# Direct loads by head groups in 512-byte pieces, GpSimd's loads between its constants, the last chunk stored in halves, and a new order of all steps

## The chip, the cores and the metric

The kernel runs on one core of a Trainium2 chip. The core has five engines with instruction queues of their own: TensorE (PE in the profile, with PEld for its weight loads), VectorE (DVE), ScalarE (ACT), GpSimd (POOL) and SyncE (SP). Transfers between the chip's memory and the core run on 16 DMA engines and are issued here from SP, ACT and POOL. The metric is the device time of one execution in microseconds (us).

## The reference

Causal attention over 4 batches, 8 heads, 768 positions and a head size of 64, in which three heads see all earlier positions and five see the first 4 positions and a window of 64. Its output, 3072 rows of 512, goes through a gated feed-forward layer with a gated residual:

```python
scores = scale * np.matmul(q, k.transpose(0, 1, 3, 2))
stream_keep = causal & (is_sink | in_win)
mask = np.where(retr[0, :, 0, 0, None, None], full_mask, stream_mask)
...
a = a / (np.sum(a, axis=-1, keepdims=True) + 1e-09)
x = np.matmul(a, v)            # heads put side by side: 3072 x 512
g = x @ w_gate
gelu = 0.5 * g * (1.0 + erf(g * inv_sqrt2))
ffn_out = gelu * (x @ w_val) @ w_out
res_gate = 1.0 / (1.0 + np.exp(-(x @ w_res)))
out = x + res_gate * ffn_out
```

The weights are 512 x 1536 (gate, value), 1536 x 512 (out) and 512 x 512 (res).

## The kernel before

**Stages.** The 3072 rows are worked on in six chunks of 512 (`CHUNKS`, line 25), each four tiles of 128 positions. A chunk goes through attention (scores on PE, exponentials on ACT, masks on DVE, products with the values on PE, normalization on DVE), then gate and value products (PE), GELU (ACT), their product (DVE), then the output product and the residual gate. From chunk 1 on, half of the gate and value products and all output products are Strassen-like: sums of blocks on DVE replace some matmuls. PE works in fp16 and sums in fp32. Heads are taken in pairs, `PAIRS = ((0, 2), (4, 6), (1, 3), (5, 7))`, in the order 0, 2, 1, 3 in the first chunks.

**The order is written out.** Each step is a task with an engine, the tasks that it depends on, and its buffers; the tasks are numbered as they are made. The list `PLAN` (line 51) names them by number in the order in which they enter their engines' queues, with a letter where a task may run on several engines (a: ACT, d: DVE, g: POOL), and `w34` for 34 filler matmuls on zeros (line 1468). `PLACES` gives the buffer of each. `schedule` (line 263) puts the tasks into the queues, and `assign_waits` gives each one the semaphore waits that its dependences need. Nothing is decided while the kernel runs: an engine waits where its next task is not ready.

**The front.** The numbers that matter:

- 211, 217 (SP) and 214, 220 (ACT) are the direct loads (`loads_first`, line 646): keys and queries of batch 0, positions 0 to 255, in fp32. In the kernel before, 211 and 214 bring positions 0 to 127 of all eight heads, 217 and 220 positions 128 to 255. A contiguous piece in memory is one head's row of 64 numbers, 256 bytes.
- 212, 213, 215, 216, 218, 219, 221, 222 cast them to fp16 in halves. 223, 225, 227, 229 transpose them on PE, 224, 226, 228, 230 copy the results to the tiles kT and qT.
- 417, 420, 423, 428 are the scores of pairs 0, 2, 1 and 3 of the first two tiles, and 418, 421, 424/425, 429 their exponentials (line 911).
- 231, 232 are GpSimd's loads of the keys and queries of positions 256 to 511, with their transposes and copies 245 to 252. 233 to 236 load the values, 254 a piece of the keys of batch 1.
- 2, 4 to 11 are GpSimd's nine constants: the identity (2) and two masks. Here every load from GpSimd depends on all of them (`consts` in `dma`, line 540). 12 copies a part of the window mask, 3 makes the fp32 identity. 237 to 240 copy sink values.
- 200, 202, 204 load `w_gate` in three pieces, 201, 203, 205 `w_val`, 206 `w_res`, 207 to 210 `w_out`. 507 and 490 cast attention outputs to fp16 on GpSimd. 575 is the first product that needs load 204.

In the queues before, GpSimd runs all constants, then 232, 231, 233, 234, 236, 235, 254, 200, 201, 203, the sink copies, 202, 204, 205, and so on; the casts 507 and 490 come after 206.

**The back.** Of the last chunk, `output_fast` (line 1340) runs for two pairs of tiles, `pi` 0 and 1. Each pair has two residual products with tanh (1799 to 1802 for `pi` 0), seven Strassen products, DVE's sums (`plus`; 1814, 1817, 1820), gates (`gated`, line 1409), adds of x (line 1419, DVE or GpSimd) and stores (line 1425, SP or ACT). 1821 and 1822 are the very last product; it needs sum 1817. `end` marks the pair that is gated, added and stored in halves of 256 columns: before, `pi` 1 of the last chunk alone, while the pair that finishes last in the list, `pi` 0, is added and stored in whole rows.

**xD** (line 1101) are transposing copies within the core on SP's queue, one in each of chunks 3 to 5 (1188, 1424, 1662).

Of the kernel before, what the change touches and what calls it, by code (L numbers as in the profile page):

```python
# [429 lines left out]
def build_kernel(nc, q, k, v, w_gate, w_val, w_out, w_res, out):  # L430
# [61 lines left out]
    def at16(buf):  # L492
        return at(buf).bitcast(FP16)
# [152 lines left out]
    def loads_first(b, a):  # L646
# [18 lines left out]
        for i in range(2):  # L665
            for j in (1, 0):
# [17 lines left out]
                for p in range(NPAIR):  # L684
                    (BB.ktok if j else BB.qtok)[p, a + i] = t
# [881 lines left out]
```

## Time and profile before

| what | us |
|---|---|
| median of 3 runs | 259.19 (259.07 to 259.86) |
| the profiled execution | 259.19 |
| its span, first to last instruction | 257.4 |
| PE busy | 250.4 |
| DVE busy | 203.1 |
| ACT busy | 164.7 |
| POOL busy | 105.5 |

A line of a timeline or of the page's groups gives start or count, duration, engine, the line of the kernel, the operation and its tiles, and in brackets how long the engine had been idle before and what ended that. "x16" is the number of merged instructions, and the duration is that of all of them. A window's row gives its length, then for PE, PE's weight loads, DVE, ACT and POOL the busy time and the number of instructions, then the granted clock, the share of the DMA engines and GB/s. The chain of work that ended last is followed back from the last instruction, at each step to what released it; a line of it names the engine that was waited for. Matmuls are pipelined and their ends are modelled, so that a PE that shows as busy can still be waiting a little.

### The profile page before, as it was taken

How to read it: one execution, taken by the hardware profiler on the slowest of the kernel's cores; microseconds unless marked ns; L12 is line 12 of the kernel's file. 1: busy time of each engine (PE TensorE's matmuls, PEld its weight loads, DVE VectorE, ACT ScalarE, POOL GpSimd, SP SyncE). 2: the span in 40 equal slices, each digit the busy share in tenths (PEclk: the TensorE clock that was granted, in tenths of full speed). 3: DMA queues.
4: the chain of work that ended last, by engine and by line, in shares of the span. 5: the costliest groups of instructions: out<-in, count | busy, mean ns of one | idle time of the engine just before them, and what ended most of it. 6: DMA issues, size and time to landing. Idle time of an engine off the chain costs nothing.

```text
span 257.4 us, 8048 instructions
## 1 busy us (share of the span) xinstructions
PE 250.4 (97%) x3407; PEld 176.7 (69%) x3407; DVE 203.1 (79%) x453; ACT 164.7 (64%) x298; POOL 105.5 (41%) x144
## 2 busy tenths in 40 slices
PE   8999999999999999999999999999999999999992
PEld 5657645468576668567678566689587689678881
DVE  2798344899988997577998478999687887768975
ACT  2698944986567994475977355993456997264410
POOL 8995900947862549069423086003310010210031
PEclk9999999999999999999999999999999999999999
DMA  8999999999999999999929899409997005360004
GB/s 150 170 199 206 194 198 203 162 154 106 172 154 248 179 114 125 176 247 168 147 34 162 224 138 153 29 10 83 150 154 239 3 6 84 41 84 4 3 22 144
DMA packets 104116, 33.71 MB, mean 131 GB/s; under 512 B 90768, under 2 KB 99216, under 8 KB 104080
## 3 DMA queue, kind: packets, MB, share of 16 engines
q0 software_dynamic: 72592, 18.36, 82.3%
q1 hardware_dynamic: 29120, 13.91, 28.4%
q10 hardware_dynamic: 2368, 0.92, 1.6%
q8 instruction: 27, 0.44, 0.7%
q14 instruction: 9, 0.07, 0.1%
HBM read 29.36 MB, written 10.49 MB: 155 GB/s over the span
## 4 chain that ended last, share of the span: by engine, by line
PE 93%; ACT 3%; DVE 2%; issue 1%; DVEq 0%
PE ps L477 49%; PE ps L478 32%; PE ps L895 5%; PE ps L1468 3%; PE ps L1019 2%; PE ps L1115 1%; PE ps L726 1%; PE ps L986 1%; ACT es L911 1%; ACT ea L911 1%; DVE otile L1409 1%; ACT vs L622 0%; PE ps L670 0%; DVE otile L1385 0%; DVE otile L1419 0%
## 5 line engine op out<-in xcount | busy, mean ns | idle before, releaser
L1413 POOL DMA_DIRECT2D out_dram<-otile x16 | 15.8, 1021 | 85.8 <-DVE otile L1409 55.3
L542 POOL DMA_DIRECT2D qks<-in_q_dram x35 | 33.8, 1010 | 16.6 <-issue 8.3
L542 POOL DMA_DIRECT2D qks<-in_k_dram x35 | 34.4, 1034 | 12.8 <-PE ps L726 12.8
L477 PE MATMUL ps<-xT,wg 128*128 128x512 f16 (+1 forms) x172 | 38.4, 337 | 0.0
L477 PE MATMUL ps<-xT,wv 128*128 128x512 f16 (+1 forms) x166 | 37.9, 338 | 0.0
L1183 ACT ACTIVATE gact<-ps 128x512 f16<-128x512 f32 x38 | 22.1, 595 | 23.8 <-PE ps L477 16.3
L1185 DVE SCALAR_TENSOR_TENSOR hT<-gact,ps 128x512 f16<-128x512 f16 x38 | 25.7, 684 | 11.6 <-ACT gact L1183 6.1
L1257 DVE TENSOR_TENSOR ps<-ps,otile 128x256 f32<-128x256 f32 x60 | 24.9, 431 | 9.9 <-PE ps L478 5.1
L542 POOL DMA_DIRECT2D va<-in_v_dram x24 | 24.5, 1055 | 5.1 <-PE ps L477 5.1
L477 PEld LDWEIGHTS ps<-xT,wg 128*128 128x128 f16 x172 | 16.4, 98 | 11.0 <-ACT gact L1183 0.3
L1353 ACT ACTIVATE srs<-ps 128x512 f32<-128x512 f32 x22 | 13.1, 597 | 15.3 <-PE ps L478 11.6
L477 PEld LDWEIGHTS ps<-xT,wv 128*128 128x128 f16 x166 | 15.9, 98 | 9.9 <-ACT xT L1125 0.3
L1275 ACT ACTIVATE gact<-ps 128x512 f16<-128x512 f32 x30 | 16.9, 598 | 6.7 <-PE ps L478 4.1
L911 ACT ACTIVATE ea<-ps 128x1024 f16<-128x1024 f32 (+2 forms) x24 | 21.1, 928 | 0.0
L1282 DVE SCALAR_TENSOR_TENSOR hT<-gact,ps 128x512 f16<-128x512 f16 x30 | 19.6, 680 | 1.7 <-PE ps L477 1.7
L1253 ACT ACTIVATE ps<-ps 128x256 f32<-128x256 f32 x25 | 9.2, 370 | 16.9 <-PE ps L477 12.2
L478 PE MATMUL ps<-xT,wv 128*64 128x512 f16 (+1 forms) x156 | 19.2, 341 | 0.0
L1086 DVE TENSOR_TENSOR xtok<-ps,rcp 128x512 f32<-128x512 f32 (+1 forms) x28 | 17.1, 609 | 1.0 <-ACT x L1094 0.4
L477 PE MATMUL ps<-wo,hT 128*128 128x256 f16 (+1 forms) x114 | 17.7, 296 | 0.0
L478 PE MATMUL ps<-xT,wg 128*64 128x512 f16 (+1 forms) x144 | 17.3, 344 | 0.0
L1385 DVE TENSOR_TENSOR otile<-otile,ps 128x256 f32<-128x256 f32 x33 | 13.6, 415 | 4.6 <-PE ps L478 3.6
L895 PE MATMUL ps<-qT,kT 64*128 64x64 f16 (+3 forms) x391 | 16.5, 213 | 0.7 <-ACT xT L1125 0.6
(188 smaller groups left out, 588.0 us busy)
## 6 DMA issues: line engine op xcount, KB each, us to landing
out_dram<-xtok SPq DMA_DIRECT2D x4, 1024.0 KB, 5.7
out_dram<-otile POOLq DMA_DIRECT2D x16, 256.0 KB, 4.8
va<-in_v_dram POOLq DMA_DIRECT2D x24, 128.0 KB, 6.7
qks<-in_q_dram POOLq DMA_DIRECT2D x32, 64.0 KB, 6.2
qks<-in_k_dram POOLq DMA_DIRECT2D x32, 64.0 KB, 6.4
wg<-in_moe_w_gate_dram POOLq DMA_DIRECT2D x3, 512.0 KB, 12.3
wv<-in_moe_w_val_dram POOLq DMA_DIRECT2D x3, 512.0 KB, 12.2
wo<-in_moe_w_out_dram POOLq DMA_DIRECT2D x4, 384.0 KB, 18.5
```

The source lines that it names most:

```text
L477: return e.matmul(o, lhsT=lhsT, rhs=rhs, **k)
L478: return [e.matmul(o[h:h + 64], lhsT=lhsT[:, h:h + 64], rhs=rhs, **k) for h in (0, 64)][-1]
L542: return G.add(eng, issue, lambda e: e.dma_start(out_ap(), in_ap), list(deps) + (consts if eng == "pool" else []), prio, bufs=bufs, dma=co ...
L895: return [e.matmul(at(scr)[:, oo:oo + w], lhsT=side(BB, qb, low, 1)[half, k0:k0 + 128], rhs=side(BB, qb, low, 0)[half, qq:qq + w], start=T ...
L911: return e.activation(out=o, in_=i_, func=AF.Exp, scale=SM_SCALE)
L1086: t2 = G.add("dve", c_dve(2 * n * 64), lambda e: e.tensor_tensor(out=xview(), in0=avv(0, DHEAD), in1=scale(), op=ALU.mult), [t1] + xdeps, ...
L1183: ta = G.add("act", c_act(512), (lambda gb=gb, ga=ga, gw=gw: lambda e: e.activation(out=at(ga)[:, :], in_=at(gb)[:, gw], func=AF.Gelu))(), ...
L1185: th = G.add("dve", c_dve(512), (lambda vb=vb, ga=ga, f=f, vw=vw: lambda e: e.scalar_tensor_tensor(out=hv(f), in0=at(ga)[:, :], scalar=0.5 ...
L1257: return G.add("dve", c_dve(256), lambda e: e.tensor_tensor(out=at(ps)[:, o], in0=at(ps)[:, BL], in1=at(es)[:, 0:256], op=ALU.add), deps, ...
L1275: ta = G.add("act", c_act(512), (lambda x=x, ga=ga, both=both: lambda e: e.activation(out=two(at(ga)[:, :]), in_=both(x), func=AF.Gelu))() ...
L1282: th = G.add("dve", c_dve(512), (lambda x=x, f=f, ga=ga, both=both: lambda e: e.scalar_tensor_tensor(out=two(hv(f)), in0=two(at(ga)[:, :]) ...
L1413: t = G.add("pool", 1.0, (lambda ot=ot, r0=r0: lambda e: e.dma_start(out[r0:r0 + 128, :], at(ot)[:, :], accum_op=ALU.add))(), ends + [stor ...
```

## The change

- **Direct loads.** 211 and 214 now bring heads 0 to 3 of positions 0 to 255, 217 and 220 heads 4 to 7. Two neighbouring positions of a head are one piece of 512 bytes on one partition. The transposes take every second position and the copies put them in order. On SP 211 now goes first. Scores 417 and 420 thereby depend on 211 and 214 alone, 423 and 428 on 217 and 220.
- **GpSimd.** Its loads no longer depend on the constants. The queue is 6, 7, 231, 8, 232, 2, 233, 4, 234, 9, 235, 10, 11, cast 221, 236, 5, 200, 237, 238, 201, 239, 240, 202, 203, cast 507, 264, 204, 205, ..., 254, ..., 206. Computations on GpSimd depend on the computation before them there, and its transfers on the latest xD ahead of them in the list.
- **The last chunk.** `end` holds for both pairs, so that `pi` 0 has one more gate, two more adds and two more stores (numbers from 1823 on, with 1830 to 1865 moved up by five). Two dependences of the products on tanh and on each other are gone.
- **The order.** `PLAN` and `PLACES` are new throughout. 21 fillers instead of 34 stand ahead of the first transposes, 31 instead of 47 in all. On ACT, 224, 219, 222, 12 come ahead of exponential 418, and 228, 252 and 3 are its own now; 246 has gone to DVE. At the end, 1817 is queued ahead of 1820 on DVE, and 1815, 1816 ahead of 1818, 1819 on PE.

```diff
 PLAN = (
-    "0 17 18 214 217 211 1 220 199 212a 216 6 7 15 218a 16 2 215 8 w34 225 219a 4 3 213 223 226 9 10 222 5 227 221a 228 229 "
...
+    "0 15 211 214 6 7 18 220 231 199 212a 8 232 217 17 1 213a 2 215 216a w21 223 233 225 4 16 226 224a 234 219a 9 235 222a "
...
+    "1868g 1800 1814 1823 1818 1825g 1817 1870 1819 1801 1821 1822 1820 1827 1869a 1824 1826 1802 1829 1828a 1864a 1831g "
+    "1833 1830 1832 1834a "
...
+            if e == "pool" and t.dma:
+                t.deps += [u for u in order if u.name == "xD"][-1:]
+            if e == "pool" and not t.dma:
+                t.deps += [u for u in prog[e] if not u.dma][-1:]
...
-        return G.add(eng, issue, lambda e: e.dma_start(out_ap(), in_ap), list(deps) + (consts if eng == "pool" else []), prio,
+        return G.add(eng, issue, lambda e: e.dma_start(out_ap(), in_ap), list(deps), prio,
...
-        for i in range(2):
+        for o in range(2):
             for j, src, eng in ((1, k, "sp"), (0, q, "act")):
-                ld = G.add(eng, 0.6, (lambda src=src, j=j, i=i: lambda e: e.dma_start(
-                    view(j, i, 0, 2).rearrange("p (h d) -> p h d", h=NHEAD),
-                    src[b, :, lo + 128 * i:lo + 128 * i + 128, :].rearrange("h p d -> p h d")))(),
+                ld = G.add(eng, 0.6, (lambda src=src, j=j, o=o: lambda e: e.dma_start(
+                    view(j, o, 0, 2).rearrange("p (h w) -> p h w", h=4),
+                    src[b, 4 * o:4 * o + 4, lo:lo + 256, :].rearrange("h (p i) d -> p h (i d)", i=2)))(),
...
-                    for p in range(NPAIR) for x in range(2)])(),
+                    for m, p in enumerate(ps_) for i in range(2) for x in range(2)])(),
...
-        end = c == len(CHUNKS) - 1 and pi == 1
+        end = c == len(CHUNKS) - 1
...
-        p6 = product(X, "S2", "T2", False, [k1] + (tas if end else []))
+        p6 = product(X, "S2", "T2", False, [k1])
...
-        p4 = [product(X, "A22", "T4", False, [c22] + ([p2] if end else []))]
+        p4 = [product(X, "A22", "T4", False, [c22])]
```

The copies of the sink values may now stand on GpSimd by the list instead of always, the clearing of the sink tiles and the mask products are written in the form for several engines with DVE as the only one, and the gates that read from SBUF alone have a name of their own.

More of the change, by code (lines that the diff above doesn't have):

```diff
@@ L534, in build_kernel @@
     for i, vk in enumerate(P_vk.items):
-        P_vk.last[i] = [G.add("dve", 0.5, (lambda vk=vk: lambda e: e.memset(vk[:, :, :], 0.0))(), [t_blank], -94, name="vzero")]
+        P_vk.last[i] = [G.flex({e_: (0.5, (lambda vk=vk: lambda e: e.memset(vk[:, :, :], 0.0))()) for e_ in ("dve",)}, [t_blank], -94, name="vzero")]
     for i, va in enumerate(P_v.items):
@@ L541, in dma @@
         issue = 0.85 if eng == "pool" else 1.2
-        return G.add(eng, issue, lambda e: e.dma_start(out_ap(), in_ap), list(deps) + (consts if eng == "pool" else []), prio,
+        return G.add(eng, issue, lambda e: e.dma_start(out_ap(), in_ap), list(deps), prio,
                      bufs=bufs, dma=cost, name=name, grp=grp)
     inits = [x for l in P_v.last for x in l], [x for l in P_vk.last for x in l]
-    consts = [x for x in G.tasks if x.name == "const"]
     wtok = {}
@@ L609, in values @@
                 if b == 0:
-                    t.eng, t.alts, t.prio = "pool", None, VK_AT
-                    t.dur, t.deps = 0.3, t.deps + [x for x in G.tasks if x.name == "const"]
+                    t.prio = VK_AT
+                    hs = VK[BB.vktok.index(t)]
+                    t.alts["pool"] = (0.3, vk("pool", BB.vktok.index(t), *hs))
         a_ = max(a, 1)
@@ L651, in loads_first @@
         st, half = [Buf(P_st), Buf(P_st)], [Buf(P_x16), Buf(P_x16)]
-        view = lambda j, i, o, n=1: at(st[j])[:, :].bitcast(FP32)[:, (i * 2 + o) * 256:(i * 2 + o + n) * 256]
-        h16 = lambda j, i, o, n=1: at(half[j]).rearrange("p c i k -> p (c i k)")[:, (i * 2 + o) * 256:(i * 2 + o + n) * 256]
-        for i in range(2):
+        view = lambda j, o, g, n=1: at(st[j])[:, :].bitcast(FP32)[:, (o * 2 + g) * 256:(o * 2 + g + n) * 256]
+        h16 = lambda j, o, g, n=1: at(half[j]).rearrange("p c i k -> p (c i k)")[:, (o * 2 + g) * 256:(o * 2 + g + n) * 256]
@@ L659, in loads_first @@
                     [], -60, bufs=[st[j]], dma=0.9, name="ldf")
-                for o in range(2):
-                    def cast(on, j=j, o=o, i=i):
-                        return lambda e: (e.activation(out=h16(j, i, o), in_=view(j, i, o), func=AF.Copy) if on == "act" else
-                                          e.tensor_copy(out=h16(j, i, o), in_=view(j, i, o)))
-                    tok[j, i, o] = G.flex({e: (0.4, cast(e)) for e in ("dve", "act", "pool")}, [ld], -205, bufs=[st[j], half[j]], name="c16")
@@ L665, in loads_first, with cast @@
-        for i in range(2):
+                for g in range(2):
+                    def cast(on, j=j, o=o, g=g):
+                        return lambda e: (e.activation(out=h16(j, o, g), in_=view(j, o, g), func=AF.Copy) if on == "act" else
+                                          e.tensor_copy(out=h16(j, o, g), in_=view(j, o, g)))
+                    tok[j, o, g] = G.flex({e: (0.4, cast(e)) for e in ("dve", "act", "pool")}, [ld], -205, bufs=[st[j], half[j]], name="c16")
+        for o in range(2):
+            ps_ = sorted(ORDER[2 * o:2 * o + 2])
+            assert sorted(h for p in ps_ for h in PAIRS[p]) == list(range(4 * o, 4 * o + 4))
@@ L666, in loads_first @@
             for j in (1, 0):
                 scr = Buf(P_ps, "scr0")
-                to, o0 = (BB.kt, lo + 128 * i) if j else (qb, qo + 128 * i)
-                tt = G.add("pe", 0.3, (lambda scr=scr, j=j, i=i: lambda e: [
-                    e.transpose(out=at16(scr)[64 * x:64 * x + 64, p * 128:(p + 1) * 128],
-                                in_=h16(j, i, 0, 2)[:, PAIRS[p][x] * 64:PAIRS[p][x] * 64 + 64], identity=ident[:, :])
-                    for p in range(NPAIR) for x in range(2)])(),
-                    [t_ident] + [tok[j, i, o] for o in range(2)], 80 * i - 205, bufs=[half[j], scr], name="qkT")
+                to, o0 = (BB.kt, lo) if j else (qb, qo)
@@ new lines, in loads_first @@
+                tt = G.add("pe", 0.3, (lambda scr=scr, j=j, o=o, ps_=ps_: lambda e: [
+                    e.transpose(out=at16(scr)[64 * x:64 * x + 64, (m * 2 + i) * 128:(m * 2 + i + 1) * 128],
+                                in_=h16(j, o, 0, 2)[:, PAIRS[p][x] % 4 * 128 + i * 64:PAIRS[p][x] % 4 * 128 + i * 64 + 64], identity=ident[:, :])
+                    for m, p in enumerate(ps_) for i in range(2) for x in range(2)])(),
+                    [t_ident] + [tok[j, o, g] for g in range(2)], 80 * o - 205, bufs=[half[j], scr], name="qkT")
@@ L674, in loads_first, with ev @@
                 tt.mode = "col"
-                def ev(on, scr=scr, to=to, o0=o0):
+                def ev(on, scr=scr, to=to, o0=o0, ps_=ps_):
                     def fn(e):
-                        o = at(to)[:, :, o0:o0 + 128]
-                        i_ = at16(scr)[:, 0:512].rearrange("c (m w) -> c m w", m=NPAIR)
+                        o = at(to)[:, ps_[0]:ps_[1] + 1:ps_[1] - ps_[0], o0:o0 + 256].rearrange("c m (p i) -> c m p i", i=2)
+                        i_ = at16(scr)[:, 0:512].rearrange("c (m i p) -> c m p i", m=2, i=2)
@@ L680, in fn @@
                         return e.tensor_copy(out=o, in_=i_) if on == "dve" else e.activation(out=o, in_=i_, func=AF.Copy)
                     return fn
-                t = G.flex({"dve": (c_dve(512), ev("dve")), "act": (c_act(512), ev("act"))}, [tt], 80 * i - 205,
+                t = G.flex({"dve": (c_dve(512), ev("dve")), "act": (c_act(512), ev("act"))}, [tt], 80 * o - 205,
                            bufs=[scr, to], name="qkE")
-                for p in range(NPAIR):
-                    (BB.ktok if j else BB.qtok)[p, a + i] = t
+                for p in ps_:
+                    for i in range(a, a + 2):
+                        (BB.ktok if j else BB.qtok)[p, i] = t
@@ L946, in scores @@
                 mt = t_win if P.c else t_win0
-            tm = G.add("dve", c_dve(w * L, 1.8 if L == 2 else 1.5, False), (lambda view=view, m_=m_, split=split: lambda e: e.tensor_tensor(
-                out=split(view()), in0=split(view()), in1=m_, op=ALU.mult))(), txs + mt, pr + (85 if P.c == 0 and p in ORDER[:2] else -90), bufs=[P.et], name=f"mask{p}")
+            alts = {"dve": (c_dve(w * L, 1.8 if L == 2 else 1.5, False), (lambda view=view, m_=m_, split=split: lambda e: e.tensor_tensor(
+                out=split(view()), in0=split(view()), in1=m_, op=ALU.mult))())}
+            tm = G.flex(alts, txs + mt, pr + (85 if P.c == 0 and p in ORDER[:2] else -90), bufs=[P.et], name=f"mask{p}")
             for x in xs:
@@ L1410, in output_fast @@
                     out=at(ot)[:, w], in0=at(sr)[:, w], scalar=1.0, in1=at(src or ot)[:, w], op0=ALU.add, op1=ALU.mult))(),
-                    [tas[i]] + deps, pr + (len(ends) - 40 if end else 0), bufs=[sr, ot] + ([src] if src else []), name="gated"))
+                    [tas[i]] + deps, pr + (len(ends) - 40 if end else 0), bufs=[sr, ot] + ([src] if src else []), name="gated" if src else "gate2"))
             if c in ACCUM and not end:
```

149 rows, old and new, of tables (PLACES, PLAN) are left out of this document.

## The prediction

> **What bounds the kernel now.** I read the page first, then the chain that ended last in order of time, then the timelines of the two ends, engine by engine.
>
> ```profile
> PE 250.4 (97%) x3407; PEld 176.7 (69%) x3407; DVE 203.1 (79%) x453; ACT 164.7 (64%) x298; POOL 105.5 (41%) x144
> ```
>
> ```profile
> 20.62 0.32 PE ps L1019 x14
> 20.93 2.81 PE ps L477 x37
> ...
> 250.32 0.02 issue
> 250.34 0.43 DVE otile L1385
> ```
>
> The 97% hides the structure; the chain shows it. From 20.62 to 250.32 every step of it is PE: the core goes from one matmul to the next, and what other engines do there costs nothing. Ahead of that it is not PE that is waited for, as the rows below show, and after it the chain stands on DVE and a store. The 230 us between hold a fixed number of matmuls, so the time is when the unbroken stream starts, plus its length, plus what follows its end. The change acts on the first and the last, and sets a new order for the middle.
>
> The front, on ACT, DVE and PE (start, duration, engine, line):
>
> ```profile
> 7.25 1.33 ACT L662 ACTIVATE x<-qks 128x256 f16<-128x256 f32 x4 [3.66 <-DMA qks<-in_k_dram]
> 8.63 0.60 ACT L680 ACTIVATE kT<-ps 128x512 f16<-128x512 f16 x1
> 10.44 0.60 ACT L911 ACTIVATE es<-ps 128x512 f16<-128x512 f32 x1 [1.22 <-PE ps L895]
> ...
> 17.09 1.09 ACT L911 ACTIVATE es<-ps 128x512 f16<-128x512 f32 x2 [0.52 <-PE ps L895]
> ...
> 20.77 1.28 ACT L1137 ACT_TABLE_LOAD   x1
> ```
>
> ```profile
> 5.46 0.48 DVE L663 CAST x<-qks 128x256 f16<-128x256 f32 x1 [3.79 <-DMA qks<-in_q_dram]
> ...
> 9.88 0.46 DVE L508 COPY m_win<-m_win 128x256 f16<-128x256 f16 x1
> ```
>
> ```profile
> 1.12 6.81 PE L1468 MATMUL ps<-blank 128*128 128x256 f16 x34 [1.12 <-DVE blank L511]
> ...
> 9.09 0.41 PE L670 MATMUL ps<-ident,x 128*64 128x128 f16 x8 [0.27 <-DVE x L663]
> 9.43 0.72 PE L1468 MATMUL ps<-blank 128*128 128x256 f16 x5
> 10.11 0.46 PE L895 MATMUL ps<-qT,kT 64*128 64x64 f16 x15
> ```
>
> Until 7.25 ACT waits for keys. The first exponential runs at 10.44, and from there ACT is busy almost without a gap until the table load at 20.77, 10.33 us later, where the stream of products begins. DVE is as full: in the row of this window it is the third engine, with 4.85 of 5 us (the last column is GB/s).
>
> ```profile
> 15.00:20.00 5.00, 4.24 (x81) 2.79 (x79) 4.85 (x17) 4.29 (x10) 4.80 (x6) 1.00 1.26 206
> ```
>
> **The direct loads.** For the four loads of line 656 the trace gives their spread:
>
> ```profile
> DMA to landing us min/median/max: 4.0/5.3/6.5
> ```
>
> They are issued between 0.8 and 1.3 (two each on SP and ACT), so the first lands near 4.8 and the last near 7.8. Each brings 128 rows of all eight heads, so the first scores need all four. After the change each brings four heads over 256 rows, and scores 417 and 420 (heads 0 to 3) need only 211 and 214, the first on SP's and on ACT's queue. That holds whatever a 512-byte piece costs. I take the keys at 4.8 and the queries at 5.46, where DVE's cast shows them now.
>
> From there: four casts, three of them on ACT (1.33 / 4 = 0.33 each), end near 6.1. 21 fillers of 6.81 / 34 = 0.20 us end near 5.4, so they don't hold PE up. A group of eight transposes takes 0.41, or up to twice that at the rate of the early fillers (0.20 each against 0.72 / 5 = 0.14 or less at 9.43). The queries' group then ends between 6.6 and 7.0. The copy (0.46, as the one at 9.88) and the scores (10.44 - 10.11 = 0.33) make 7.4 to 7.8. But ACT has work queued ahead of exponential 418: the copy of kT (0.60), two more casts (0.66) and the window-mask copy taken from DVE (0.46 there), after keys transposed near 6.5. I take 8.2 against 10.44: **2.2 us earlier**, by ACT's queue, because the rows add up there with nothing beside them. Bounds: 1.6 (half-rate array and that queue behind it) and 2.8 (the queue hidden).
>
> ```profile
> 2.00:4.00 2.00, 2.00 (x11) 1.45 (x10) 0.00 (x0) 1.49 (x2) 1.62 (x8) 1.00 0.92 209
> ```
>
> While these loads move in 256-byte pieces the core gets 209 GB/s; nothing of the trace of before shows the same load in larger ones. The Trainium skill, "DMA: Bandwidth & Descriptors", Specifications, gives 512 B as the smallest transfer at line rate, with a read-modify-write below. By the page the first pair would land some tenths sooner, and the time would be near 256.3.
>
> **How much reaches the stream.** ACT's 10.33 us gain copy 228 (0.60) and the float copy of the identity (0.3, below the 0.46 of a mask copy twice as wide); copy 252 comes as its like 246 goes. Against this +0.9 stand its gaps, 0.52 the largest, while DVE is eased by what ACT takes over. Net +0.5, between +0.2 and +0.9. So the stream starts 2.2 - 0.5 = **1.7 us earlier**, bounds 0.7 and 2.6.
>
> **GpSimd.** Its nine constants ran before all its loads:
>
> ```profile
> 3.82 1.10 POOL L542 DMA_DIRECT2D qks<-in_q_dram  x1 [0.32 <-POOL m_win L497]
> ...
> 22.75 0.74 POOL L1095 CAST x<-xtok 128x256 f16<-128x256 f32 x2 [2.94 <-DVE xtok L1086]
> ```
>
> Its first load now goes after two constants, near 1.6, and all four values go ahead of any weight, with load 254 out of their way. The identity comes two loads of some 1.1 us later, near 4.0; the casts hide that until 5.4, and past that each tenth would be a tenth of the front. The constants of the window mask end near 8, with loads between them; ACT's mask copy wants them near 7.8, so 0.2 us could show, within the bounds. The order added among GpSimd's own computations is the order they stand in: nothing.
>
> The added wait: GpSimd's transfers wait for the latest xD transpose ahead of them in the list; there are three:
>
> ```profile
> xT<-x SPq DMA_TRANSPOSE x3, 3.9
> ```
>
> Queued behind are loads of batch 3 and the adding stores. The nearest load (378) feeds a transposing load 61 places further on, about 9 us at 257 us for 1,695 places; the landing's 3.9 us fit in. I put it at nothing; without this cover, at most 3.9 once.
>
> **The middle.** Nearly every place is new, the work the same. An order wins or loses PE's waits on others, and the largest of those for products in the list of waits is:
>
> ```profile
> PEld ps L477 <- DVE ps L1257: 2.1, 9, 0.4
> ```
>
> I take zero, with 1.0 either way: half of it won, or half as much added.
>
> **The last chunk**, on GpSimd, DVE, PE, PE's weight loads and ACT:
>
> ```profile
> 248.49 2.21 POOL L1419 TENSOR_TENSOR otile<-otile,xtok 128x256 f32<-128x256 f32 x3 [22.00 <-DVE otile L1409]
> 251.63 1.27 POOL L1419 TENSOR_TENSOR otile<-otile,xtok 128x512 f32<-128x512 f32 x1 [0.94 <-DVE otile L1409]
> ```
>
> ```profile
> 251.81 1.38 DVE L1419 TENSOR_TENSOR otile<-otile,xtok 128x256 f32<-128x256 f32 x1
> 253.11 0.41 DVE L1409 SCALAR_TENSOR_TENSOR otile<-srs,otile 128x256 f32<-128x256 f32 x1
> ```
>
> ```profile
> 250.79 1.03 PE L478 MATMUL ps<-wr,xT 128*64 128x512 f16 x8
> ```
>
> ```profile
> 251.94 0.58 PEld L478 LDWEIGHTS ps<-wt,hT 128*64 128x64 f16 x12 [0.60 <-DVE otile L1385]
> ```
>
> ```profile
> 251.86 0.60 ACT L1353 ACTIVATE srs<-ps 128x512 f32<-128x512 f32 x1 [1.50 <-PE ps L478]
> 254.61 0.36 ACTq L1425 DMA_DIRECT2D out_dram<-otile  x1
> ```
>
> The last residual product ends at 251.82; the last store is issued 2.79 us later. In between, the last product waits 0.60 for sum 1817, and DVE's 256-wide add takes 1.38 beside GpSimd's 1.27 (the gate of that width takes 0.41), so the last gates start at 253.11. Now 1817 stands two products further ahead of the last one, and the 0.60 goes. What is late next is tanh 1802: 0.05 + 0.60 after the residual product. Then gate (0.41), gate (0.41) and a 256-wide add (0.41), which overlap a little: the store is issued 1.9 us after it, or 2.2 if that add has to wait for GpSimd's add 1831 (2.21 / 3 = 0.74, begun after the first gate). The rest that is new on DVE there (a sum, a gate and an add, 1.24 us) lies beside the residual product and its tanh (1.03 + 0.60). So **0.75 us less**, bounds 0.4 (a second collision) and 1.0.
>
> **The sum** is made on the profiled execution: 259.19 us with a span of 257.4, 1.8 outside, which I leave; it is also the median of the three runs. 259.2 - 1.7 - 0.75 = **256.7 us**.
>
> **The rivals.**
> - *The front gains nothing at the stream.* ACT and DVE were both full, and the earlier start is eaten by what ACT takes over and by DVE (4.85 of 5). For it: those rows. Against it: both start earlier and the sum of their work hardly grows. 259.2 - 0.75, and 0.2 for the little that is left: 258.3.
> - *A cold array.* There are 13 fillers fewer ahead of the data, and the early ones take 0.20 instead of 0.14 or less. If full rate comes only some 3 us later than now, two groups of transposes and the first scores take twice as long: 0.41 + 0.41 + 0.33, less what waits for ACT anyway, about 0.9. 257.6. Against it: the fillers, 4.3 us long, run straight into the transposes. The Trainium skill, "TensorE: Matmul & The Clock Gate", Part 1, has such a rule: half rate by default, full rate after a window of about 3.4 us of sustained work.
> - *The order wins more.* The 1.0 of the middle and 0.3 at the ends: 255.4. For it: the waits are there to be won. Against it: they are many and small.
> - *Late weights*, the slower side. The cast 507 now stands ahead of weight loads 204 and 205 on GpSimd. It waits for a norm (22.75 before, near 21.0 now); with one load of 0.8 between, 204 is issued near 22.2. Its first use, 575, comes after some 23 half products and small work, near 30.4: two matmuls each, at most 2.32 / 10 = 0.23 apiece, make 10.6 us, and I add 1.0 for the rest.
>
> ```profile
> 39.65 2.32 PE L477 MATMUL ps<-xT,wv 128*128 128x512 f16 x10
> ```
>
> ```profile
> wg<-in_moe_w_gate_dram POOLq DMA_DIRECT2D x3, 512.0 KB, 12.3
> ```
>
> At 12.3 us to landing it comes at 34.5 and PE stands 4.1 us: 260.8. It decides from 8.2 us on. Against it: the 12.3 is time behind other loads, and 512 KB at 206 GB/s take 2.5; at 22 only one weight load and one of queries are ahead.
>
> **How the numbers follow.** Forecast 0.50, nothing at the stream 0.14, cold 0.10, better order 0.14, late weights 0.12. About 0.3% (0.8 us) is what a measurement of this kernel can tell from no change, so under 258.4 is faster. 258.3 lies on that line: I count about half of its 0.14 as the same, with 0.03 of the forecast's own scatter. Faster 0.78, same 0.10, slower 0.12. The range 254.8 to 259.0 takes in the better order with half of the front's upper bound, and reaches over the case without a front gain at the high end; it leaves out late weights and a little at the low side.
>
> **What would show it.** First exponential near 8.2, table load near 19.1, first transposes after two of the four direct loads, the chain unbroken on PE from about 19 to 248.6, no wait of PE on a weight load near 30; in the tail no 0.60 before the last product, and a store issued about 2 us after the last residual product. Wrong would be: a first exponential after 9.5, a table load less than 1 us earlier, gaps of PE between 25 and 45, or a stream longer than now by over 1 us.

## The result, and the profile after

The changed kernel takes 256.93 us, the median of 4 runs (256.76 to 257.15), against 259.14 us for the kernel before in the same session (259.07 to 259.86, 4 runs). The ratio is 0.9909, with a 95% interval of 0.989 to 0.9928: faster by 0.9%. The profiled execution took 257.15 us with a span of 255.4; the one before took 259.19 with 257.4. So 2.0 us have to be found in the two traces.

The front on ScalarE (start, duration, engine, line):

```profile
7.84 0.42 ACT L513 ACTIVATE m_win<-m_win 128x256 f16<-128x256 f16 x1 [0.24 <-POOL m_win L502]
8.16 0.79 ACT L919 ACTIVATE ea<-ps 128x768 f16<-128x768 f32 x1
...
17.34 0.96 ACT L627 ACTIVATE vs<-va 64x910 f16<-64x910 f16 x1
18.20 0.63 ACT L1134 ACTIVATE xT<-ps 128x256 f16<-128x256 f32 x2
18.85 1.28 ACT L1146 ACT_TABLE_LOAD   x1
```

The first exponential runs at 8.16 instead of 10.44, and the table load at 18.85 instead of 20.77, 1.92 us earlier. The same stretch on TensorE, with its short waits, and the last products:

```profile
5.71 1.06 PE L677 MATMUL ps<-ident,x 128*64 128x128 f16 x16
...
7.57 0.46 PE L903 MATMUL ps<-qT,kT 64*128 64x128 f16 x14 [0.25 <-DVE qT L687]
...
9.33 0.64 PE L734 MATMUL ps<-ident,qks 128*64 128x128 f16 x16 [0.20 <-DMA qks<-in_k_dram]
...
10.75 0.41 PE L734 MATMUL ps<-ident,qks 128*64 128x128 f16 x8 [0.39 <-DMA qks<-in_q_dram]
...
18.44 0.19 PE L1028 MATMUL ps<-vs,es 128*64 128x65 f16 x1 [0.51 <-ACT vs L627]
...
249.40 1.06 PE L483 MATMUL ps<-wr,xT 128*64 128x512 f16 x8
250.26 0.85 PE L483 MATMUL ps<-wt,hT 128*64 128x256 f16 x12
```

The row to use is the one at 18.44. It is TensorE's last wait ahead of the end; its unbroken run begins there. In the kernel before that row is this one:

```profile
19.62 0.34 PE L895 MATMUL ps<-qT,kT 64*128 64x256 f16 x2 [0.63 <-ACT xT L1125]
```

From there to the end of the last residual product, the windows of the two kernels (stretch, its length, then the busy time of TensorE with the number of its matmuls, and of the other engines) read, before and then after:

```profile
19.62:251.82 232.20, 232.17 (x3150) 164.19 (x3150) 187.42 (x411) 152.03 (x273) 86.25 (x111) 1.00 1.12 127
```

```profile
18.44:250.46 232.02, 231.96 (x3156) 164.93 (x3158) 189.00 (x416) 147.88 (x266) 92.54 (x117) 1.00 1.08 128
```

Both runs are without a gap to 0.1 us, at a granted clock of 1.00. The unbroken run starts 1.18 us earlier and is 0.18 shorter. Who takes the table load for the start of the stream reads a gain of 1.92 and then a loss of 0.56 in the middle, which isn't there.

The last chunk after, on ScalarE, VectorE and GpSimd:

```profile
250.49 0.60 ACT L1362 ACTIVATE srs<-ps 128x512 f32<-128x512 f32 x1 [1.58 <-PE ps L483]
...
251.13 1.87 ACTq L1434 DMA_DIRECT2D out_dram<-otile  x3
```

```profile
251.12 0.42 DVE L1418 SCALAR_TENSOR_TENSOR otile<-srs,otile 128x256 f32<-128x256 f32 x1
251.47 0.41 DVE L1418 SCALAR_TENSOR_TENSOR otile<-srs,ps 128x256 f32<-128x256 f32 x1
...
251.91 0.72 DVE L1428 TENSOR_TENSOR otile<-otile,xtok 128x256 f32<-128x256 f32 x1
```

```profile
251.63 0.72 POOL L1428 TENSOR_TENSOR otile<-otile,xtok 128x256 f32<-128x256 f32 x1 [1.30 <-DVE otile L1418]
```

The last residual product ends at 250.46, the last add at 252.63: the last store can be issued 2.17 us after that product, where it was 2.79. The sum of the three: 1.18 + 0.18 + 0.62 = 1.98 us of the 2.0 between the spans.

### The profile page after: what moved, and what is told of

Read it like the earlier page. It is cut to its first block, busy times and chain, and to the rows that moved or that the text cites. A ratio compares the mean times of both kernels' runs of the same rounds, so it can differ in the third digit from the quotient of the medians.

```text
span 255.4 us, 8042 instructions
## 1 busy us (share of the span) xinstructions
PE 248.1 (97%) x3395; PEld 175.5 (69%) x3395; DVE 202.7 (79%) x455; ACT 162.2 (63%) x295; POOL 106.0 (42%) x146
## 3 DMA queue, kind: packets, MB, share of 16 engines
q10 hardware_dynamic: 1776, 1.18, 1.5%
## 4 chain that ended last, share of the span: by engine, by line
PE 90%; DMA 3%; DVE 3%; ACT 1%; POOL 1%; issue 1%; POOLq 0%
PE ps L482 48%; PE ps L483 33%; PE ps L903 5%; DMA va<-in_v_dram 3%; PE ps L1028 2%; PE ps L1124 1%; DVE xtok L1095 1%; PE ps L734 1%; PE ps L995 1%; POOL qks L547 0%; ACT vs L627 0%; POOL m_win L502 0%; DVE x L1104 0%; DVE otile L1418 0%; DVE otile L1428 0%
## 5 line engine op out<-in xcount | busy, mean ns | idle before, releaser
L547 POOL DMA_DIRECT2D qks<-in_k_dram x35 | 31.4, 991 | 29.6 <-DMA qT<-qks 18.1
L547 POOL DMA_DIRECT2D qks<-in_q_dram x35 | 31.1, 997 | 3.2 <-DMA qT<-qks 3.2
L482 PE MATMUL ps<-wo,hT 128*128 128x256 f16 (+1 forms) x114 | 18.9, 296 | 0.0
L903 PE MATMUL ps<-qT,kT 64*128 64x64 f16 (+4 forms) x391 | 16.1, 213 | 0.5 <-DVE qT L687 0.3
```

Source lines behind the costliest of these rows:

```text
L482: return e.matmul(o, lhsT=lhsT, rhs=rhs, **k)
L547: return G.add(eng, issue, lambda e: e.dma_start(out_ap(), in_ap), list(deps), prio, bufs=bufs, dma=cost, name=name, grp=grp)
L903: return [e.matmul(at(scr)[:, oo:oo + w], lhsT=side(BB, qb, low, 1)[half, k0:k0 + 128], rhs=side(BB, qb, low, 0)[half, qq:qq + w], start=T ...
```

## The experiments

All ratios are to the kernel before in the same session; the changed kernel stands at 0.9909 (0.989 to 0.9928). Offsets between two traces compare the start of the same instruction of one engine in both. A diff of `PLAN` shows only the entries around the change; "..." stands for lines left out.

| kernel | us, median (range, runs) | ratio (95% interval) |
|---|---|---|
| grouped loads alone, old order | 259.03 (258.87 to 259.65, 12) | 0.9992 (0.9982 to 1.0003) |
| constants first | 257.75 (257.46 to 258.18, 6) | 0.9936 (0.992 to 0.9952) |
| direct loads split, 512 bytes | 258.45 (257.74 to 260.4, 12) | 0.9973 (0.9955 to 0.9992) |
| direct loads split, 256 bytes | 259.44 (258.66 to 259.84, and one of 641 that the ratio leaves out, 12) | 0.9998 (0.9986 to 1.0009) |
| 8 fillers | 259.18 (258.33 to 260.03, 12) | 0.9997 (0.9983 to 1.0011) |
| first pair whole | 257.92 (257.63 to 258.16, 5) | 0.9949 (0.9936 to 0.9962) |
| old order of the last products | 257.16 (256.73 to 257.35, 4) | 0.9917 (0.9905 to 0.993) |
| one shifted copy on GpSimd | 258.59 (257.21 to 259.73, 12) | 0.9968 (0.995 to 0.9985) |
| the changed kernel again | 257.04 (256.87 to 257.38, 4) | 0.9912 (0.9899 to 0.9925) |
| old order, last chunk changed | 264.66 (263.1 to 265.77, 6) | 1.0201 (1.0172 to 1.0229) |
| last add on VectorE | 257.18 (257.1 to 257.3, 4) | 0.9916 (0.9903 to 0.9929) |
| both shifted copies on GpSimd | 257.2 (256.54 to 259.81, 9) | 0.9929 (0.9902 to 0.9956) |

**Is it the larger pieces, or the order that they allow?** The kernel before with nothing but the regrouped loads and transposes:

```diff
-        for i in range(2):
+        for o in range(2):
...
-                    src[b, :, lo + 128 * i:lo + 128 * i + 128, :].rearrange("h p d -> p h d")))(),
+                    src[b, 4 * o:4 * o + 4, lo:lo + 256, :].rearrange("h (p i) d -> p h (i d)", i=2)))(),
```

> The kernel before with only the direct loads and their transposes regrouped by heads in 512-byte pieces, in the old order. Theory (the grouping saves time only because the new order starts the first scores after two of the four loads): the old order still runs all four transposes ahead of the first scores, so the first exponential stays within 0.6 us of 10.44 us and the time within 0.6 us of 259.1. Rival (the larger pieces themselves bring the data sooner): first exponential at 9.2 us or earlier and 257.9 us or less.

259.03 us, no gain that can be told from zero. The landing of the four direct loads, and ScalarE:

```profile
DMA to landing us min/median/max: 3.8/4.6/5.4
```

```profile
10.18 0.60 ACT L914 ACTIVATE es<-ps 128x512 f16<-128x512 f32 x1 [1.55 <-PE ps L898]
```

Before, landing took 4.0/5.3/6.5. The same bytes in 512-byte pieces arrive up to 1.1 us sooner, and ScalarE's casts start at 6.23 instead of 7.25; yet the first exponential moves by 0.26 us only, because the old order runs all four groups of transposes first. (The Trainium skill, "DMA: Bandwidth & Descriptors", Specifications, names 512 B as the smallest transfer at line rate; the landing agrees with it, the time doesn't follow.) The piece size alone is worth nothing here; what uses it is the order.

**And within the new order?** A load of 256-byte pieces over the same rows and heads is two DMAs, so its partner has two as well:

```diff
...
-                    view(j, o, 0, 2).rearrange("p (h w) -> p h w", h=4),
-                    src[b, 4 * o:4 * o + 4, lo:lo + 256, :].rearrange("h (p i) d -> p h (i d)", i=2)))(),
+                    view(j, o, g, 1).rearrange("p (h w) -> p h w", h=2),
+                    src[b, 4 * o + 2 * g:4 * o + 2 * g + 2, lo:lo + 256, :].rearrange("h (p i) d -> p h (i d)", i=2)) for g in range(2)])(),
```

> The changed kernel with each of the four direct loads issued as two DMAs of two heads each, still in 512-byte pieces; the partner of the next run. Both theories: each queue issues twice as often, so 256.9 to 257.6 us.

```diff
...
-                    view(j, o, 0, 2).rearrange("p (h w) -> p h w", h=4),
-                    src[b, 4 * o:4 * o + 4, lo:lo + 256, :].rearrange("h (p i) d -> p h (i d)", i=2)))(),
+                    view(j, o, 0, 2).rearrange("p (h i d) -> p h i d", h=4, i=2)[:, :, i, :],
+                    src[b, 4 * o:4 * o + 4, lo + 128 * i:lo + 128 * i + 128, :].rearrange("h p d -> p h d")) for i in range(2)])(),
...
```

> As the run before, but each of the two DMAs of a load takes half of the rows of four heads, in 256-byte pieces, and the copies out of the transposes write plain rows. Theory (the grouping by heads gives the gain, the piece size does not): within 0.3 us of the run with 512-byte pieces, and the copies back at about 0.42 us instead of 0.69. Rival (the piece size gives the gain): 0.5 us or more above it, with the direct loads landing at least 0.5 us later.

258.45 and 259.44 us (259.35 without the one of 641): the first is above what I expected of it, and the second lies 0.9 above the first, as the rival had it. The rival's other sign is missing: with 256 bytes the loads land only 0.2 to 0.4 us later. Landing, first with 512 and then with 256 bytes:

```profile
DMA to landing us min/median/max: 2.7/4.2/6.3
```

```profile
DMA to landing us min/median/max: 3.0/4.4/6.7
```

The traces don't give the 0.9 to the pieces, though. With 256 bytes the first exponential comes 0.42 later (9.90 against 9.48), but the table load only 0.05 later (20.12 against 20.07): the copies that are plain again (0.42 us on VectorE instead of 0.69) give a part of it back; where the rest is made up wasn't followed. The profiled executions end 0.6 apart because of one stall of TensorE near 133 us, in the waits of TensorE of the 256-byte kernel (engine, line, waited for: us, times, longest):

```profile
PE ps L483 <- issue: 0.7, 1, 0.7
```

A good part of the 0.9 goes with TensorE's granted clock, which is on record for every execution. With 256 bytes nine of eleven executions have a mean clock of 0.993 or less (258.97 to 259.84 us), with 512 bytes five of twelve (258.41 to 260.40). The others, at 0.995 or more, take 258.66 and 259.12 with 256 bytes and 257.74 to 258.54 with 512. Both profiled executions are of this second kind, so neither trace shows the fall; the run with both shifted copies on GpSimd, below, does.

What I claimed, that the piece size doesn't matter, stands at the stream's start (0.05) and not at the first exponential (0.42); whether the pieces make the clock fall more often, or cause the stall, is open. What both runs show is that splitting a load costs in this order: the second pair is now issued as late as 2.4 us, behind GpSimd's first load (1.55), ScalarE waits 1.96 for it (8.55), and the table load comes 1.2 us later than in the changed kernel.

**GpSimd's loads between its constants.** Undone by moving the loads 231 to 235 behind the constants in the order:

```diff
-220 231 199 212a 8 232 217 17 1 213a 2 215 216a w21 223 233 225 4 16 226 224a 234 219a 9 235 222a w4 417 420 10 11 12a 218 221g 227 229 230 418 236 5 w2
+220 199 212a 8 217 17 1 213a 2 215 216a w21 223 225 4 16 226 224a 219a 9 222a w4 417 420 10 11 5 231 232 233 234 235 12a 218 221g 227 229 230 418 236 w2
```

> The changed kernel with GpSimd's loads put behind all its constants again. Theory (the front's transfers share one rate, and the early issue is only cover): 256.9 to 257.4 us, first exponential at 8.2 us still. Rival (the early issue is a good part of the gain): 257.9 us or more, with waits of TensorE on keys or queries near 9 to 11 us grown by 1 us or more.

257.75 us, between the two. The table load is at 19.32, 0.47 later than in the changed kernel, and GpSimd and TensorE show why:

```profile
8.72 0.46 POOL L668 CAST x<-qks 128x256 f16<-128x256 f32 x1
```

```profile
9.24 0.41 PE L677 MATMUL ps<-ident,x 128*64 128x128 f16 x8 [0.75 <-POOL x L668]
```

It isn't the landing of the transfers alone: GpSimd's own cast 221 (7.95 in the changed kernel) stands behind the first five loads, which now begin at 4.14 instead of 1.55; it comes 0.8 later, and TensorE waits 0.75 for it. The first exponential even comes 0.32 earlier (7.84), since the window's constants are ready sooner; it says nothing of the stream here. The other 0.6 us that this profile loses come with one stall of TensorE at 132.5. So putting the loads between the constants is worth about 0.5 us at the table load, which has no term in the prediction's sum.

**The fillers.**

```diff
-216a w21 223
+216a w8 223
```

> The changed kernel with 8 instead of 21 filler products ahead of the first transposes. Theory (the fillers warm the array, and the new order keeps enough of them): the transposes and first scores take 0.3 to 1 us longer, the first exponential comes at 8.3 to 9.2 us, and the time is 257.1 to 258.0 us. Rival (the array's state at 5 us does not matter to the end): 256.6 to 257.0 us.

259.18 us, the whole gain gone. The first exponential stays at 8.16, as neither theory had it, but TensorE is slow long after it:

```profile
7.61 0.72 PE L903 MATMUL ps<-qT,kT 64*128 64x128 f16 x14
8.26 1.06 PE L677 MATMUL ps<-ident,x 128*64 128x128 f16 x16
...
9.79 1.06 PE L734 MATMUL ps<-ident,qks 128*64 128x128 f16 x16
```

The 14 scores take 0.72 against 0.46 in the changed kernel, and the transposes at 9.79 take 1.06 against 0.64. The windows' granted clock doesn't show it (third number from the right, 1.00). The trace's clock record begins only where the full rate does, at 11.25 us here and at 6.71 in the changed kernel, and what lies ahead of it counts as 1.00:

```profile
8.00:10.00 2.00, 2.00 (x34) 1.33 (x30) 0.63 (x1) 2.00 (x4) 1.94 (x4) 1.00 2.17 165
```

The table load comes 0.74 later (19.59). Most of what this profile loses beyond that, 2.4 us by the offsets on either side, comes with two stops of TensorE late in the run, of 1.29 and 0.70, of which this is the first:

```profile
215.24 1.05 PE L483 MATMUL ps<-va,ea 128*64 128x65 f16 x54 [1.29 <-issue]
```

The fastest of its 12 runs, 258.33, is still 1.6 above the fastest of the changed kernel; the trace gives 0.74 of a loss to the front, and the rest isn't explained by the array's rate. The cold-array rival was a real danger: 8 fillers are too few and 21 are enough. Nothing between was run.

**The halves of the last chunk.** Undone for the first pair of tiles, with the entries renumbered:

```diff
-            parts = [(slice(256, 512), None, [c12]), (slice(0, 256), None, [c11])] if i == 0 and end else \
+            parts = [(slice(256, 512), None, [c12]), (slice(0, 256), None, [c11])] if i == 0 and end and pi == 1 else \
...
-            for w, deps in [(p[0], [t_]) for p, t_ in zip(parts, ends)] if end else [(slice(0, 512), ends)]:
+            for w, deps in [(p[0], [t_]) for p, t_ in zip(parts, ends)] if end and pi == 1 else [(slice(0, 512), ends)]:
```

> The changed kernel with the first pair of tiles of the last chunk added and stored whole again (only the last pair in halves). Theory (the end is set by the last pair, behind the last residual product, and the earlier pair's stores are beside that): within 0.4 us of 256.9 us. Rival (the halves give the gain of the last chunk): 257.5 us or more.

257.92 us: the rival. GpSimd and VectorE at the end:

```profile
250.63 1.26 POOL L1428 TENSOR_TENSOR otile<-otile,xtok 128x512 f32<-128x512 f32 x1 [1.70 <-DVE otile L1418]
```

```profile
250.83 1.35 DVE L1418 SCALAR_TENSOR_TENSOR otile<-srs,otile 128x256 f32<-128x256 f32 x1 [0.27 <-ACT srs L1362]
```

VectorE's gate of 256 columns takes 1.35 us instead of 0.42: it ends at 252.18, 0.29 after GpSimd's add has ended at 251.89. The last add ends 3.07 us after the last residual product (253.23 - 250.16) instead of 2.17. So the halves are worth 0.9 us by themselves: not because stores start sooner, but because what GpSimd holds VectorE up with at the very end is 0.72 long and not 1.26 (the gate alone loses 0.93). The Trainium skill, "SBUF — State Buffer", SBUF: two separate sides, says that a VectorE operation with two inputs in SBUF and a GpSimd operation that reads SBUF lock each other out for a whole instruction; the two ends agree, as do those of the changed kernel's last add (0.28 us after GpSimd's), and so does the gate at 251.47 of the changed kernel, which has one operand in PSUM and takes its 0.41 across the start of GpSimd's add.

**The order of the last products.**

```diff
-1799 1815 1816 1862g 1866 1868g 1800 1814 1823 1818 1825g 1817 1870 1819 1801 1821 1822 1820 1827
+1799 1814 1818 1819 1815 1816 1862g 1866 1868g 1800 1823 1825g 1820 1817 1870 1801 1821 1822 1827
```

> The changed kernel with the last chunk's products 1818 and 1819 put ahead of 1815 and 1816 again, as in the kernel before. Theory (the old order makes the last product wait for VectorE's copy): a wait of TensorE of 0.4 to 0.8 us shortly ahead of the last products returns, and the time is 257.2 to 257.8 us. Rival (the wait is covered by the last tile's tail anyway): 256.7 to 257.0 us.

257.16 us: no loss that can be told. The edit also puts 1820 ahead of 1817 on VectorE again, as in the kernel before. Of the wait this is left, on TensorE's weight loads and not on its products:

```profile
PEld ps L483 <- DVE otile L1394: 0.3, 1, 0.3
```

So neither the order of these products nor that of the two sums is what removed the 0.60, and the wait was no term of its own: in the kernel before, the product that waited ended at 252.79 (251.94 + 0.85), still ahead of the last gates at 253.11, which stood behind VectorE's add of 1.38.

**Whose add is last?**

```diff
-1829 1828a 1864a 1831g 1833
+1829 1831 1828a 1864a 1833
```

> The changed kernel with GpSimd's last add (0.72 us, begun at 251.63 us) put on VectorE ahead of the last gate, so that nothing of GpSimd runs beside the last adds. Theory (VectorE's 256-wide add takes 0.72 us there instead of 0.42 only because GpSimd runs, so GpSimd's add saves nothing): the last add takes about 0.42 us and the end comes within 0.15 us of the changed kernel's. Rival (GpSimd's add is real help): the end comes 0.3 us later or more; the other rival (the collision costs more than the add): 0.3 us earlier or more.

257.18 us. The last add:

```profile
252.21 0.42 DVE L1428 TENSOR_TENSOR otile<-otile,xtok 128x256 f32<-128x256 f32 x1
```

Without GpSimd it takes 0.42, and ends 2.33 us after the last residual product (which ends at 250.30) instead of 2.17: 0.16, just outside the 0.15 that the theory allowed. One more add on VectorE costs about what the collision cost; with this work in the tail nothing is to be had by moving that add.

**Can the unbroken run start sooner?** The shifted copy at 17.34, for which TensorE waits last, moved to GpSimd, behind the weight loads 202 and 203:

```diff
-461 243a 508
+461 202 203 243g 508
```

> The changed kernel with ScalarE's copy of shifted values at 17.34 us moved to GpSimd, which is idle from 15.46 to 20.36 us. Theory (TensorE's unbroken run starts at its last wait, 0.51 us for this copy at 17.93 us, and what starts it sooner comes off the time): run starts 0.2 to 0.5 us earlier and the time is 256.4 to 256.7 us. Rival (TensorE would wait there for the masks or the feature copies anyway, or GpSimd slows VectorE): 256.8 to 257.3 us.

```profile
14.58 0.94 POOL L627 COPY vs<-va 64x910 f16<-64x910 f16 x1
```

```profile
18.41 0.22 PE L1028 MATMUL ps<-vs,eb 128*64 128x65 f16 x1 [0.24 <-DVE xtok L1095]
```

The rival's wait is there: TensorE stands 0.24 for VectorE's normalised rows. Against the changed kernel's trace the whole run is offset by -0.34 us at 15 us, ahead of the moved copy, and still by -0.32 at 20. The copy gained nothing: the changed kernel without an edit, below, has nearly the same offset (-0.28). The profiled run was one of the fastest of twelve (257.37 against a median of 258.59). What the others lose goes with the granted clock: the five executions at 0.996 or more took 257.21 to 258.04 us, the seven at 0.993 or less 258.41 to 259.73. Then both copies:

```diff
-475 244 470 485 486 487 471 445 447 488 489 460 461 243a 508
+475 470 485 486 487 471 445 447 488 489 460 461 202 203 244g 243g 508
```

> As the run with one copy of shifted values on GpSimd, but with VectorE's copy of them (0.40 us at 17.27 us) there too. Theory (with one copy moved, TensorE's last wait was for VectorE, so both engines have to be relieved): the wait of 0.24 us for VectorE's normalised rows near 18.2 us goes, TensorE's unbroken run starts 0.3 to 0.5 us earlier than in the changed kernel, and the fastest runs come to 256.2 to 256.5 us. Rival (TensorE is held there by its own work or by the feature copies): 256.7 us or more in the fastest runs.

```profile
14.07 2.02 POOL L627 COPY vs<-va 64x910 f16<-64x910 f16 x2
```

```profile
14.15 1.13 DVE L955 TENSOR_TENSOR es<-es,m_win 128x512 f16<-128x512 f16 x1
```

The fastest run, 256.54, is 0.2 below the fastest of the changed kernel, but the median is not. In the profile GpSimd's copies hold a mask of VectorE up (1.13 instead of 0.41) and TensorE waits 0.97 for it. What follows costs more than the wait. The two stretches of this profile around 16.87, and the first of them in the changed kernel:

```profile
13.46:16.87 3.41, 2.13 (x57) 1.43 (x56) 3.34 (x11) 2.35 (x6) 2.46 (x3) 1.00 1.24 205
16.87:20.28 3.41, 3.41 (x46) 2.82 (x47) 2.60 (x9) 2.16 (x5) 0.00 (x0) 0.50 1.24 206
```

```profile
13.46:16.87 3.41, 3.19 (x75) 2.06 (x72) 3.34 (x13) 3.26 (x8) 1.93 (x4) 1.00 1.19 185
```

TensorE is busy for 2.13 us of the first stretch instead of 3.19, and in the second its granted clock is 0.50 (third number from the right). Six fp32 matmuls take 1.52 there instead of 0.85, and the offset to the changed kernel grows from 0.5 us ahead of it to 1.24 behind it. This was one of the three executions of nine at a mean clock of 0.993 or less (258.38 to 259.81); the six others took 256.54 to 257.31, with a median of 256.93, level with the changed kernel. None of the changed kernel's eight executions is below 0.996. So moving work to GpSimd here gains nothing and sometimes leaves TensorE idle enough for its clock to be halved; that the idle time is what halves it is read from this one trace and wasn't tested. No version that I tried beats the changed kernel in the median.

**The last chunk by itself.** The changed code and its last 85 entries, behind the old order; the ends of the two lists:

```diff
...
-1810 1811 1849 1850 1851 1855 1857g 1812 1852 1853 1813 1799 1860 1814 1818 1859a 1800 1861 1819 1815 1816 1820 1801
-1802 1862g 1823 1856g 1824g 1817 1863 1858 1864 1865 1821 1826 1822 1827 1828 1825 1829a
...
+1868g 1800 1814 1823 1818 1825g 1817 1870 1819 1801 1821 1822 1820 1827 1869a 1824 1826 1802 1829 1828a 1864a 1831g
+1833 1830 1832 1834a
```

> The changed kernel's code and its order of the last chunk alone (its last 85 entries), behind the old order of everything earlier. It differs from the run of the grouped loads alone (259.03 us) by the last chunk. Theory (the last chunk's halves and order are worth 0.6 us by themselves, the rest is the front): 258.3 to 258.6 us. Rival (the last chunk gives nothing without the front's order): 258.9 us or more; the other rival (it gives most of the gain): 257.9 us or less.

264.66 us, and none of the expectations: the run doesn't tell what the last chunk is worth, since it brought another term to light. Longest waits of GpSimd, ScalarE and VectorE, between 140 and 154 and between 180 and 195 us:

```profile
POOL qks L547 <- DMA xT<-x: 17.6, 1, 17.6
...
ACT otile L1262 <- DMA out_dram<-otile: 2.2, 1, 2.2
...
POOL qks L547 <- DMA xT<-x: 6.0, 1, 6.0
...
DVE otile L1263 <- DMA out_dram<-otile: 2.9, 1, 2.9
```

```profile
153.15 0.39 PE L482 MATMUL ps<-xs,wg 128*128 128x256 f16 x2 [1.86 <-DVE ps L1266]
...
194.56 0.41 PE L483 MATMUL ps<-xs,wg 128*64 128x256 f16 x4 [2.65 <-DVE ps L1266]
```

This is the wait that the change adds: a load of GpSimd waits for the latest transposing DMA. In the old order it stands 17.6 us there, the adding stores behind it are issued late, the tiles that they read come free late, and TensorE stops twice, for 4.5 us together. In the changed kernel, and by its own order, the same wait is:

```profile
POOL qks L547 <- DMA xT<-x: 4.9, 1, 4.9
```

and nobody behind it waits. The old order couldn't have carried the new rule. (The front of this kernel is also 0.85 later than with the grouped loads alone; 0.26 of it stands ahead of GpSimd's first load, 4.08 against 3.82. The rest wasn't followed up.)

**The changed kernel once more**, without an edit.

> The changed kernel once more, unedited, beside the runs of this call. Theory (front and last chunk give about 2.2 us, and what differs from run to run are single stalls of TensorE of 0.4 to 1.3 us in which it waits for nothing the profile shows): 256.7 to 257.2 us as the median, no run below 256.5, and the offset of every engine's instructions against the earlier profile constant but for such steps. Rival (the middle's pace differs between the orders): the offset drifts steadily by 0.5 us or more.

257.04 us, no run below 256.87. Against its earlier trace every instruction of ScalarE from 16 us to the end is offset by -0.26 to -0.28 us: the middle is the same to 0.02 us, and two executions differ in when GpSimd's first loads land. Issue to landing of the keys, in the earlier trace and in this one:

```profile
qks<-in_k_dram POOLq DMA_DIRECT2D x1, 256.0 KB, 7.7
```

```profile
qks<-in_k_dram POOLq DMA_DIRECT2D x1, 256.0 KB, 6.8
```

## Why the prediction was right, step by step

The prediction, 256.7 us, was right in direction, size and range. Its terms:

- **First exponential at 8.2** (8.16 measured), behind ScalarE's queue and not behind the data: right, with the 0.24 us of waiting for GpSimd's window constants that it had named.
- **The array not cold**: right in its cost with 21 fillers. Cold the array still was at first (the first 16 transposes took 1.06 in one profile of the changed kernel and 0.72 in the other, 0.64 later), but the first exponential came at 8.16 and 8.20, behind ScalarE's queue. The run with 8 puts the price of a cold array at 0.74 at the table load, near the 0.9 of that rival.
- **"That holds whatever a 512-byte piece costs"**: right for the table load (0.05 us apart with the DMAs split), not for the first exponential (0.42).
- **The stream 1.7 us earlier**: this is the term that was mis-sized, by where I read it. The table load came 1.92 earlier, but TensorE's unbroken run only 1.18 in one profile and 1.46 in the next (18.16). In the kernel before it began 1.15 ahead of the table load, in the changed one 0.41 ahead: part of ScalarE's lead was no lead of TensorE, whose last wait is for another instruction of ScalarE, the shifted copy. With the 0.18 that the run got shorter, front and middle together gave 1.36 of the 1.7.
- **GpSimd's earlier loads**: no term of the sum. The early loads, and the place of cast 221 that goes with them, are worth about 0.5 us at the table load.
- **The added wait at nothing, 3.9 at most**: right that it is covered (4.9 on GpSimd, nobody waits). That was the new order's doing: by the old one it stops TensorE for 4.5 us. The bound was too small: it took the wait for one landing, and in the old order GpSimd stands 17.6 us.
- **The middle 0 with 1.0 either way**: -0.18. In the changed kernel's two profiles the run is the same to 0.02 us; the kernel before was profiled once.
- **Late weights**: didn't come. No wait of TensorE on a weight load stands in the window from 18.44, and the gate weights landed sooner than the 12.3 us of the old profile that I feared:

```profile
wg<-in_moe_w_gate_dram POOLq DMA_DIRECT2D x3, 512.0 KB, 7.5
```

- **The last chunk 0.75**: 0.62, and it is the value with the second collision (2.2 us after the residual product; 2.17 measured). But the step by which 1817 stands two products further ahead "and the 0.60 goes" was not what gave it: with the old order of the products and sums the time is the same, while without the halves 0.9 us are lost to GpSimd's add.

Both errors have one sign: 0.34 too much for front and middle and 0.13 too much for the last chunk. They add up to the half microsecond by which the prediction of the gain (2.5) exceeds the profiled one (2.0). That they are so small is partly luck: the front's 1.36 holds some 0.5 us of GpSimd's loads for which the sum had no term, and the last chunk's size came by another step than the one named. How much of the front's gain is the grouping by heads and how much the order of the other steps, no run separates: the pieces alone gave nothing, and every run that changed them in the new order also split the loads.

## What to carry to other kernels

Where one engine runs without a gap to the end, date a change by that engine's own last wait; a milestone on another engine, even the one it waits for, can move by over half as much again (1.92 against 1.18 here). A larger DMA piece is worth what the order makes of the earlier data, so price the pair, not the piece. Near the end of a kernel keep GpSimd's operations short when VectorE works from SBUF beside them; taking the last one off GpSimd altogether gained nothing here. Look at the granted clock of every execution before comparing medians.

## What the runs showed of the hardware that I had not expected

TensorE stops now and then for 0.43 to 1.29 us with "issue" as the reason, that is, for nothing that the view of waits shows: at 132.5 us (0.43) with the constants first, at 133.1 (0.70) with the 256-byte loads, at 213.9 (1.29) with 8 fillers. In the changed kernel's profile all gaps of the unbroken run together are 0.06 us. Between such steps two executions keep their offset to a few hundredths. The traces hold a hint that I hadn't followed. The first two stops come behind the same recorded instruction of TensorE, the 3,009th, and the third exactly 2,560, ten times 256, further on. Instructions reach the core by transfers of their own; one queue carries 16 KB at a time, 27 times in the changed kernel, for the 6,866 instructions recorded of TensorE, so about 254 for each:

```profile
q8 instruction: 27, 0.44, 0.8%
```

The last such transfer ahead of the 1.29 runs from 212.93 to 213.90, and TensorE goes on at 215.24, 1.3 us after its end; in the changed kernel it has ended 2.9 us before TensorE passes that place. After the other two stops TensorE goes on 1.3 and 1.9 us after such a transfer. So these stops are probably waits for instructions; no run tests it. If so, taking out 13 fillers shifts the whole program against these transfers, and part of what the run with 8 lost is not the array's rate.

The array's slow rate at the start shows in the durations alone, with the granted clock at 1.00 throughout: with 8 fillers it was still slow at 9.79, after 4.1 us of unbroken work since 5.65, and the clock record begins at 11.25. The Trainium skill, "TensorE: Matmul & The Clock Gate", Part 1, gives about 3.4 us of sustained work, in a window that runs free of the kernel; the trace shows more here. In the 13 other traces, where the fillers start at 1.12 us, the record begins between 4.43 and 7.14, 3.3 to 6.0 us later.
